# Two weight steps' words are requested earlier at the start of a fused attention and feed-forward kernel

## The chip, the cores and the metric

One core of a Trainium2 chip runs the kernel. The metric is the device time of one execution in microseconds (us). TensorE is called PE here, VectorE DVE, ScalarE ACT, GpSimd POOL and SyncE SP; SP issues every DMA of this kernel, from one queue, in the order in which its instructions stand.

## The reference

Attention with a local window of 32 and 32 global tokens, then LayerNorm, a two-layer feed-forward with ReLU, and a residual (batch 8, 8 heads, 512 local and 32 global tokens, head width 64, model width 512, hidden width 2048):

```python
s_l = concat([scale * q_l @ k_g.T, where(|i - j| <= 32, scale * q_l @ k_l.T, -1e9)])
out_l = softmax(s_l) @ concat([v_g, v_l])          # local rows
out_g = softmax(scale * q_g @ k_all.T) @ v_all     # global rows
x = heads side by side, 8 x 544 rows of 512 
xn = (x - mean) / sqrt(var + 1e-6) * g_ln
out = x + max(xn @ w_ch1, 0) @ w_ch2
```

## The kernel before

The work is cut into chunks of 512 rows (two batch halves of 256 rows each), nine in all; the last holds the global rows. One attention **unit** is one pair of heads in one half, so a chunk has eight units: 1 to 4 give the first half, 5 to 8 the second. The units of the first chunk run alone at the start of the kernel; those of a later chunk run between the feed-forward matmuls of the chunk before.

A unit's steps: its operands `u` come by one DMA (L245, 848 KB); PE makes the scores (L262); DVE adds the mask and takes the row extremes (`p`, `mn`, L275, called the score pass below); ACT takes the exponentials (L285, four to a unit); PE transposes the result (L299) and ACT copies it (`pt`, L301); PE multiplies by the values (L317); DVE scales into `x` (L329). Behind unit 4 and behind unit 8 the half is complete: SP stores it (`xs`, L343), DVE and POOL work out the norm (L189 to L196), ACT (first half, L202) or DVE (second half, L207) applies it, and PE transposes it in four blocks (L493) that ACT and DVE write out as a high and a low part (`xh` L505, `xl` L506).

The feed-forward of a chunk runs over 16 **weight steps**. Step by step, `mm1` (L532) makes 128 hidden columns in 12 matmuls, ACT and DVE write them as two parts (L540, L541), and `mm2` (L551) adds them to the chunk's output one step later. Every weight is kept as two numbers of lower precision, and only during the start and the first chunk are they made: the words of a step (`raw`, 1 MB) come by one DMA (L165), and `split_weights` turns them into high and low parts in seven passes over 128 x 1024 elements: ACT L138 and L139, DVE L141, L142 and L146, ACT L150, DVE L152. L139 works in place on `raw` and waits only for its words; L138 also needs one of two `tmp` buffers. The words of a step lie in a staging buffer that `RAWS` names; step 5 takes that of step 1, step 6 that of step 2, step 7 that of step 3 and step 8 that of step 4, each when L146 of the earlier step has read it.

What sets the order: SP's and (from the first chunk's feed-forward on) PE's instructions are in the order of the code inside a `manual_schedule`. What stands outside the `with` block of the start (the words of step 5 and later, asked for by `split`) is merged into SP's order by the scheduler, which also orders ACT, DVE and POOL from its own estimates; all engines then run their instructions strictly in that fixed order. The start is written with `hurry(True)`, a high priority. `load_weights_to(n)` asks for the words of all steps up to n that weren't asked for yet:

```python
        for n in range(2, need[0]):
            units[n].load()
            if n == 3:
                load_weights_to(1)
...
                if n == HP + 1:
                    load_weights_to(2)
                    units[need[0]].load()
                    units[need[0] + 1].load()
```

`need[0]` is 8 and `HP` is 4. The second place stands behind the values of unit 4, and so behind the store of the first half; the words of steps 3 and 4 are asked for behind the store of the second half (`load_weights_to(4)`).

Of the kernel before, what the change touches and what calls it, by code (L numbers as in the profile page):

```python
# [46 lines left out]
def attention_ffn_kernel(  # L47
# [106 lines left out]
    def weight_stream(ap):  # L154

        ahead = []
        done = [0, 0]

        def load(n):

            for f in range(done[0], min(n, NF)):
                tag = RAWS[f]
                pool = {"w": wpool, "o": fpool}[tag[0]]
                raw = pool.tile([P, KT * P + DM], I64, name="raw", tag=tag)
                nc.sync.dma_start(raw, wd[f])  # L165
                ahead.append(raw)
                done[0] += 1

        def split(n, more=0):

            for f in range(done[1], min(n, NF)):
                load(f + 1)
                w = wpool.tile([P, 2, KT * P + DM], F32R, name="w", tag=f"w{f}")
                wts[f] = w[:, 0], w[:, 1]
                done[1] += 1
                yield from split_weights(ap, ahead.pop(0), *wts[f])
                load(f + 1 + more)

        return load, split
# [406 lines left out]
    def hurry(on):  # L586

        return tc.high_priority() if on else nullcontext()
# [5 lines left out]
    def tiles_of(xs):  # L594
        return [x[:, j, :] for x in xs for j in range(2)]
# [27 lines left out]
    load_weights_to, weights_to = weight_stream(wtmp)  # L623
# [4 lines left out]
    def begin(phase):  # L628
        if pools:
            pools.pop().__exit__(None, None, None)  # L630
        if phase == 2:
            return
        if phase == 1:
            wcm.__exit__(None, None, None)
        cm, ap = open_pool(f"apool{phase}")
        pools.append(cm)
        us = phases[phase]
        for a, b in zip(us, us[1:] + [None]):
            a.ap, a.next = ap, b
        if phase == 1:  # L640
            us[0].load_keys()
            us[0].load_values()
        else:
            us[0].load(2)
            us[1].load()
# [52 lines left out]
    with tc.manual_schedule(engines={ET.SP}):  # L698
        begin(0)
        nc.sync.dma_start(g_sb, g_ln.rearrange("(t p) o -> p (t o)", p=P))  # L700
        for n in range(2, need[0]):
            units[n].load()
            if n == 3:
                load_weights_to(1)
        with hurry(True):
            scores = [u.scores() for u in units[:need[0]]]
            after = {}
            next(scores[0])
            for n in range(need[0] + 2):
                if n < need[0]:  # L710
                    for _ in scores[n]:
                        pass
                if n + 1 < need[0]:
                    next(scores[n + 1])
                if 0 <= n - 1 < need[0]:
                    for _ in units[n - 1].transposes():
                        pass
                if n >= 2:
                    after[n - 2] = values(units[n - 2])

                if n == HP + 1:
                    load_weights_to(2)
                    units[need[0]].load()
                    units[need[0] + 1].load()
                if n == HP + 2:
                    for _ in after[HP - 1]:
                        pass
                if n == HP + 3:
                    for _ in transpose_chunk(tiles_of(ready[0][:1]), xt, 0, 4):
                        pass  # L730
            load_weights_to(4)
            for _ in after[need[0] - 1]:
                pass
            for _ in transpose_chunk(tiles_of([units[need[0] - 1].xn]), xt, 2, 4):
                pass
        for _ in weights_to(SPLIT_AHEAD):
            pass
# [122 lines left out]
```

## Time and profile before

| | us |
|---|---|
| three runs | 986.77, 989.63, 992.0 |
| median | 989.63 |
| the profiled execution's own time | 991.45 |
| its span (first to last instruction) | 989.6 |
| busy in the span: PE, DVE, ACT, POOL | 938.9, 573.7, 316.9, 44.3 |

The busy shares are an average over two very different stages: about 60 us in which the first chunk's attention runs and the weights begin to arrive, and 930 us of feed-forward in which PE hardly stops. In a row of the timeline the first number is the start, the second the duration, and the bracket tells how long the engine was idle just before and what ended that. A column PEclk gives the granted clock of PE, where 1.00 is 2.4 GHz and 0.50 is 1.2 GHz.

### The profile page before, as it was taken

The numbers are of one execution on the slowest core, as the hardware profiler recorded it, in microseconds if no ns is written. First come the engines' busy times: TensorE is split into PE (matmuls) and PEld (weight loads), VectorE is DVE, ScalarE is ACT, GpSimd is POOL, SyncE is SP. The second block draws the span as 40 slices with busy tenths as digits, with TensorE's granted clock in tenths as the row PEclk, the third lists the DMA queues.
The fourth block names the chain that finished last, engine by engine and source line by source line (L and its number), as shares of the span: only waits on it lengthen the run. The fifth ranks groups of instructions, "written<-read, shape, count | busy, mean of one in ns | idle before, by whom it ended". The sixth has DMA issues, their size and how long they took to land.

```text
span 989.6 us, 21066 instructions
## 1 busy us (share of the span) xinstructions
PE 938.9 (95%) x8616; PEld 724.4 (73%) x8616; DVE 573.7 (58%) x1873; ACT 316.9 (32%) x842; POOL 44.3 (4%) x150
## 2 busy tenths in 40 slices
PE   6579999999999999899999999999999989999997
PEld 4357777777767777777777777777777766766796
DVE  4589955666665766666666667666667542222311
ACT  5677843222322223222332232222322131232210
POOL 3000100000000000000000000000000000000000
PEclk9679999999989999999999999999999999999999
DMA  9576642422241323222233214222413244543110
GB/s 360 195 255 205 229 147 59 155 93 75 89 156 47 117 82 113 91 92 72 95 123 92 102 59 156 93 72 93 144 54 123 83 161 145 194 146 136 33 44 22
DMA packets 31872, 118.80 MB, mean 120 GB/s; under 512 B 4256, under 2 KB 6304, under 8 KB 27680
## 3 DMA queue, kind: packets, MB, share of 16 engines
q1 hardware_dynamic: 31776, 117.46, 34.6%
q8 instruction: 68, 1.11, 0.5%
q14 instruction: 28, 0.23, 0.1%
HBM read 99.62 MB, written 17.83 MB: 119 GB/s over the span
## 4 chain that ended last, share of the span: by engine, by line
PE 75%; DMA 8%; DVE 6%; SPq 2%; ACT 1%; issue 1%; POOL 0%; DVEq 0%; ACTq 0%
PE acc L551 33%; PE ph L532 32%; DMA u<-in_eu 4%; PE sc L262 3%; PE sc L317 3%; DMA raw<-in_wd 2%; DMA out<-ob 2%; SPq L560 1%; PE t L493 1%; PE pv L420 1%; DVE tmp L142 1%; DVE tmp L146 1%; PE sc L372 1%; PE t L408 1%; DVE w L152 1%
## 5 line engine op out<-in xcount | busy, mean ns | idle before, releaser
L551 PE MATMUL acc<-w,hh 128*128 128x512 f32 x1088 | 342.0, 395 | 0.0
L532 PE MATMUL ph<-xh,w 128*128 128x512 f32 (+1 forms) x1216 | 314.8, 385 | 0.0
L307 DVE STREAM_TRANSPOSE pt<-p 32x128 f32<-32x128 f32 x768 | 232.2, 302 | 38.2 <-ACT p L285 26.9
L532 PEld LDWEIGHTS ph<-xh,w 128*128 128x128 f32 x1216 | 216.3, 190 | 49.6 <-issue 2.3
L551 PEld LDWEIGHTS acc<-w,hh 128*128 128x128 f32 x1088 | 205.1, 189 | 45.4
L541 DVE SCALAR_TENSOR_TENSOR hl<-ph,hh 128x512 fp32r<-128x512 f32 (+1 forms) x144 | 93.7, 651 | 232.2 <-ACT hh L540 232.1
L551 PE MATMUL acc<-w,hl 128*128 128x512 f32 x544 | 221.8, 408 | 0.5 <-DVE hl L541 0.5
L540 ACT ACTIVATE hh<-ph 128x512 fp32r<-128x512 f32 (+1 forms) x144 | 82.3, 571 | 408.3 <-PE ph L532 408.3
L532 PE MATMUL ph<-xl,w 128*128 128x512 f32 x512 | 142.3, 400 | 0.0
L285 ACT ACTIVATE p<-p,mn 128x128 f32<-128x128 f32 x256 | 100.4, 394 | 126.1 <-DVE mn L275 125.9
L551 PEld LDWEIGHTS acc<-w,hl 128*128 128x128 f32 x544 | 102.2, 188 | 26.0 <-issue 2.6
L532 PEld LDWEIGHTS ph<-xl,w 128*128 128x128 f32 x512 | 97.1, 190 | 25.5 <-issue 1.8
L275 DVE CUSTOM_DVE_ANT_0 p<-sc,mask 128x128 f32<-128x128 f32 x256 | 63.0, 284 | 52.6 <-PE sc L262 46.9
L262 PE MATMUL sc<-u 64*32 64x128 f32 x2048 | 51.7, 297 | 22.5 <-DMA u<-in_eu 18.7
L262 PEld LDWEIGHTS sc<-u 64*32 64x32 f32 x2048 | 31.1, 113 | 46.0 <-issue 37.0
L285 ACT ACTIVATION_READ_ACCUMULATOR p<-p,mn 128x1 f32 x256 | 48.1, 188 | 0.0
L327 POOL TENSOR_SCALAR ri<-sm 128x4 f32<-128x4 f32 x64 | 16.3, 255 | 684.3 <-ACT p L285 680.6
L202 ACT ACTIVATE x<-x,rs 128x512 f32<-128x512 f32 x32 | 24.5, 809 | 54.0 <-DVE rs L196 42.0
L317 PE MATMUL sc<-u,pt 128*32 128x64 f32 x1760 | 37.2, 227 | 0.0
L317 PEld LDWEIGHTS sc<-u,pt 128*32 128x32 f32 x1760 | 28.1, 113 | 11.4 <-issue 11.2
L493 PE MATMUL t<-ident,x 128*128 128x128 f32 x136 | 23.9, 294 | 11.1 <-DVE x L207 3.9
L493 PEld LDWEIGHTS t<-ident,x 128*128 128x128 f32 x136 | 16.9, 147 | 19.0 <-issue 6.7
(61 smaller groups left out, 473.4 us busy)
## 6 DMA issues: line engine op xcount, KB each, us to landing
u<-in_eu SPq DMA_DIRECT2D x63, 848.0 KB, 5.3
raw<-in_wd SPq DMA_DIRECT2D x16, 1024.0 KB, 5.2
gk<-in_gk SPq DMA_DIRECT2D x8, 1088.0 KB, 5.1
xs<-x SPq DMA_DIRECT2D x32, 256.0 KB, 5.7
ob<-xs SPq DMA_DIRECT2D x32, 256.0 KB, 3.7
out<-ob SPq DMA_DIRECT2D x32, 256.0 KB, 2.1
gv<-in_gv SPq DMA_DIRECT2D x8, 1024.0 KB, 4.9
u<-in_eu SPq DMA_DIRECT2D x1, 512.0 KB, 3.7
```

What stands on the lines that cost most here:

```text
L202: nc.scalar.activation(x[:, j, :], x[:, j, :], AF.Identity, bias=rs[:, 1, j:j + 1], scale=rs[:, 0, j:j + 1],)
L262: nc.tensor.matmul(sc[h][gp, qb * P:(qb + 1) * P], self.e[hd, w * WIN:(w + 1) * WIN], self.e[hd, k0 * WIN:(k0 + 4) * WIN], start=True, sto ...
L275: nc.vector.tensor_tensor_reduce(out=self.p[:, c], in0=sc[h][:, qb * P:(qb + 1) * P], in1=masks[half, qb], scale=-QSCALE, scalar=BIG, op0= ...
L285: nc.scalar.activation(self.p[:, c], self.p[:, c], AF.Exp, bias=mn[:, c:c + 1], scale=-1.0, accum_out=self.sm[:, c:c + 1],)
L307: nc.vector.transpose(out=self.pt[rp, :, gp], in_=self.p[gp, :, rp])
L317: nc.tensor.matmul(pv[gp, qb * P + h * D:qb * P + h * D + D], self.pt[:, 2 * h + qb, gp], self.v[:, 4 * qb + g, h * D:(h + 1) * D], start= ...
L327: nc.gpsimd.tensor_scalar(ri, self.sm, SUM_EPS, None, ALU.add)
L493: nc.tensor.transpose(t[:, j * P:(j + 1) * P], xn[j][:, kt * P:(kt + 1) * P], ident)
L532: nc.tensor.matmul(ph[:, :n], w[:, kt, :], xx[kt][:, :n], start=(i == 0), stop=(i == 3 * KT - 1),)
L540: nc.scalar.activation(hh[:, :n], ph[:, :n], AF.Relu)
L541: nc.vector.scalar_tensor_tensor(hl[:, :n], ph[:, :n], 0.0, f32(hh[:, :n]), ALU.max, ALU.subtract)
L551: nc.tensor.matmul(acc[t], a[:, ts], w, start=(f == 0 and i == 0), stop=(f == NF - 1 and i == 2),)
```

## The change

The words of step 2 are asked for right behind the operands of unit 8, and those of step 3 where those of step 2 were, behind the first half's store:

```diff
             units[n].load()
             if n == 3:
                 load_weights_to(1)
+        load_weights_to(2)
         with hurry(True):
             scores = [u.scores() for u in units[:need[0]]]
             after = {}
@@
                 if n == HP + 1:
-                    load_weights_to(2)
+                    load_weights_to(3)
                     units[need[0]].load()
                     units[need[0] + 1].load()
```

The words of step 4 stay behind the second half's store. No instruction is added or taken away on PE, DVE or ACT; what moves is their order. Three places show it. A name's number is that of a buffer: `raw_151` holds the words of step 1 in both kernels, `raw_488` before and `raw_161` now those of step 2, `raw_675` and `raw_490` those of step 3, `raw_677` step 4, `raw_745` step 5, `raw_747` step 6, `raw_804` step 7, `raw_903` step 8.

SP, from the operands of unit 8 (`u_159`) on; `x_283` or `x_285` is the first half, `x_530` or `x_532` the second, and the two `u` behind them belong to the next chunk. Before:

```order
L245 DMA u_159<-in_eu 128x1696
L165 DMA raw_745<-in_wd 128x1024
L343 DMA xs_132<-x_283 128x512 x2
L165 DMA raw_488<-in_wd 128x1024
L245 DMA u_490<-in_eu 128x1696
L245 DMA u_492<-in_eu 128x1696
L165 DMA raw_747<-in_wd 128x1024
L343 DMA xs_132<-x_530 128x512 x2
L165 DMA raw_675<-in_wd 128x1024
L165 DMA raw_677<-in_wd 128x1024
```

Now:

```order
L245 DMA u_159<-in_eu 128x1696
L165 DMA raw_161<-in_wd 128x1024
L165 DMA raw_745<-in_wd 128x1024
L165 DMA raw_747<-in_wd 128x1024
L343 DMA xs_132<-x_285 128x512 x2
L165 DMA raw_490<-in_wd 128x1024
L245 DMA u_492<-in_eu 128x1696
L245 DMA u_494<-in_eu 128x1696
L165 DMA raw_804<-in_wd 128x1024
L343 DMA xs_132<-x_532 128x512 x2
L165 DMA raw_677<-in_wd 128x1024
L165 DMA raw_903<-in_wd 128x1024
```

Step 2's words moved ahead, and with them those of step 6, which now stand ahead of the first half's store, and those of step 7, ahead of the second half's.

ACT, between the copy of unit 4's transposes (`pt_391`, now `pt_393`) and the end of the first half; `p_372` or `p_374` are the exponentials of unit 6, `p_429` or `p_431` of unit 7, `p_504` or `p_506` of unit 8. Before:

```order
L301 COPY pt_391<-tp_392 128x512
L139 ACTIVATE raw_745<-raw_745 128x1024
L285 ACTIVATE p_372,sm_371<-p_372,mn_370 128x128 x4
L301 COPY pt_448<-tp_449 128x512
L285 ACTIVATE p_429,sm_428<-p_429,mn_427 128x128 x4
L301 COPY pt_523<-tp_524 128x512
L202 ACTIVATE x_283<-x_283,rs_479 128x512 x2
L285 ACTIVATE p_504,sm_503<-p_504,mn_502 128x128 x4
L301 COPY pt_562<-tp_563 128x512
L138 ACTIVATE tmp_711<-raw_488 128x1024
L139 ACTIVATE raw_488<-raw_488 128x1024
```

Now:

```order
L301 COPY pt_393<-tp_394 128x512
L138 ACTIVATE tmp_711<-raw_161 128x1024
L139 ACTIVATE raw_161<-raw_161 128x1024
L285 ACTIVATE p_374,sm_373<-p_374,mn_372 128x128 x4
L301 COPY pt_450<-tp_451 128x512
L139 ACTIVATE raw_745<-raw_745 128x1024
L150 CAST w_710<-tmp_711 128x1024
L285 ACTIVATE p_431,sm_430<-p_431,mn_429 128x128 x4
L301 COPY pt_525<-tp_526 128x512
L139 ACTIVATE raw_747<-raw_747 128x1024
L285 ACTIVATE p_506,sm_505<-p_506,mn_504 128x128 x4
L202 ACTIVATE x_285<-x_285,rs_481 128x512 x2
```

Ahead of unit 6's exponentials stand two passes in place of one, ahead of unit 7's two more, and ahead of unit 8's the in-place pass on step 6's words; the two passes of the first half's norm moved from ahead of unit 8's exponentials to behind them, and behind those come `pt_564` and the two passes of step 3 in the place of step 2's. On DVE, step 2's L141, L142 and L146 now stand ahead of unit 7's score pass.

DVE, from the second half's first two blocks to the score pass of unit 9 (`p_751`, the next chunk's first); `tmp_720` belongs to step 3 before, `tmp_737` to step 4, `tmp_796` to step 5. Before:

```order
L506 SCALAR_TENSOR_TENSOR xl0_594<-t_681,g_sb_87,xh0_593 128x256
L506 SCALAR_TENSOR_TENSOR xl0_594<-t_686,g_sb_87,xh0_593 128x256
L141 TENSOR_SCALAR tmp_720<-tmp_720 128x1024
L142 SCALAR_TENSOR_TENSOR tmp_720<-tmp_720,raw_675 128x1024
L506 SCALAR_TENSOR_TENSOR xl2_606<-t_691,g_sb_87,xh2_605 128x256
L506 SCALAR_TENSOR_TENSOR xl2_606<-t_696,g_sb_87,xh2_605 128x256
L146 SCALAR_TENSOR_TENSOR tmp_720<-raw_675,tmp_720 128x1024
L141 TENSOR_SCALAR tmp_737<-tmp_737 128x1024
L142 SCALAR_TENSOR_TENSOR tmp_737<-tmp_737,raw_677 128x1024
L275 ISA p_751,mn_749<-sc_752,mask00_96 128x128
```

Now:

```order
L506 SCALAR_TENSOR_TENSOR xl0_596<-t_681,g_sb_87,xh0_595 128x256
L506 SCALAR_TENSOR_TENSOR xl0_596<-t_686,g_sb_87,xh0_595 128x256
L141 TENSOR_SCALAR tmp_737<-tmp_737 128x1024
L142 SCALAR_TENSOR_TENSOR tmp_737<-tmp_737,raw_677 128x1024
L141 TENSOR_SCALAR tmp_796<-tmp_796 128x1024
L146 SCALAR_TENSOR_TENSOR tmp_737<-raw_677,tmp_737 128x1024
L506 SCALAR_TENSOR_TENSOR xl2_608<-t_691,g_sb_87,xh2_607 128x256
L506 SCALAR_TENSOR_TENSOR xl2_608<-t_696,g_sb_87,xh2_607 128x256
L142 SCALAR_TENSOR_TENSOR tmp_796<-tmp_796,raw_745 128x1024
L152 TENSOR_TENSOR w_736<-tmp_737,w_736 128x1024
L146 SCALAR_TENSOR_TENSOR tmp_796<-raw_745,tmp_796 128x1024
L275 ISA p_751,mn_749<-sc_752,mask00_96 128x128
```

Step 4 is now where step 3 was, and its L146 and the L141 of step 5 moved from behind the last two blocks to ahead of them. On ACT, L138 of step 5 likewise moved ahead of the last two `xh`, and the in-place pass on the words of step 8 (`raw_903`) moved ahead of unit 9's exponentials.

## Rows read from the trace of the kernel before

**Rows 1.** Three stretches of the span: the stretch, its length, then busy us (and instructions) of PE, of PE's weight loads, of DVE, ACT and POOL, the granted clock of PE, the busy share of the DMA engines and their GB/s.

```profile
0.00:60.00 60.00, 34.91 (x593) 21.81 (x594) 30.67 (x111) 36.15 (x97) 12.27 (x54) 0.78 0.70 269
60.00:160.00 100.00, 96.94 (x883) 74.51 (x882) 78.46 (x168) 65.85 (x133) 6.00 (x11) 0.98 0.56 188
160.00:760.00 600.00, 587.82 (x5152) 459.61 (x5151) 393.02 (x1379) 163.84 (x499) 21.34 (x69) 0.99 0.30 98
```

**Rows 2.** The timeline of all engines from the second half's store to the first matmul of the feed-forward.

```profile
48.04 0.80 SPq L343 DMA_DIRECT2D xs<-x  x2
...
54.17 1.12 ACT L138 ACTIVATE tmp<-raw 128x1024 f32<-128x1024 f32 x1 [1.02 <-DMA raw<-in_wd]
...
56.21 0.83 ACT L505 ACTIVATE xh<-t,g_sb 128x256 fp32r<-128x256 f32 x2
56.35 1.23 DVE L142 SCALAR_TENSOR_TENSOR tmp<-tmp,raw 128x1024 int32<-128x1024 int32 x1 [0.34 <-ACT raw L139]
...
57.50 0.87 DVE L506 SCALAR_TENSOR_TENSOR xl<-t,g_sb,xh 128x256 fp32r<-128x256 f32 x2
...
58.03 1.49 PE L262 MATMUL sc<-u 64*32 64x128 f32 x32 [3.55 <-DVE xl L506]
...
59.45 0.80 PE L532 MATMUL ph<-xh,w 128*128 128x512 f32 x1
```

**Rows 3.** The timeline of SP's DMA issues, to 50 us: `u` are units' operands, `raw` a step's words.

```profile
4.17 4.72 SPq L245 DMA_DIRECT2D u<-in_eu  x4
20.74 0.33 SPq L165 DMA_DIRECT2D raw<-in_wd  x1
...
33.04 0.45 SPq L165 DMA_DIRECT2D raw<-in_wd  x1
...
44.21 0.33 SPq L165 DMA_DIRECT2D raw<-in_wd  x1
...
48.89 0.95 SPq L165 DMA_DIRECT2D raw<-in_wd  x2
```

**Rows 4.** DMA issues, by size and by the time from issue to landing (the last number, in us), each asked for one short stretch: 8.5 to 9 us (unit 8's operands), then 20.7 to 21, 33 to 33.4, 44 to 44.5 and 48.8 to 49.3 us (the words of steps 5, 2, 6 and 3).

```profile
u<-in_eu SPq DMA_DIRECT2D x1, 848.0 KB, 16.9
...
raw<-in_wd SPq DMA_DIRECT2D x1, 1024.0 KB, 7.0
...
raw<-in_wd SPq DMA_DIRECT2D x1, 1024.0 KB, 5.1
...
raw<-in_wd SPq DMA_DIRECT2D x1, 1024.0 KB, 4.7
...
raw<-in_wd SPq DMA_DIRECT2D x1, 1024.0 KB, 5.3
```

**Rows 5.** The timeline of ACT: the in-place pass on step 5's words, the first exponentials of units 6 and 7, the norm of the first half, the first exponential of unit 8, and step 2's passes around the first half's blocks.

```profile
27.86 1.10 ACT L139 ACTIVATE raw<-raw 128x1024 int32<-128x1024 uint16 x1 [2.43 <-DMA raw<-in_wd]
28.86 0.39 ACT L285 ACTIVATE p<-p,mn 128x128 f32<-128x128 f32 x1
...
31.29 0.40 ACT L285 ACTIVATE p<-p,mn 128x128 f32<-128x128 f32 x1 [0.32 <-DVE mn L275]
...
35.05 1.52 ACT L202 ACTIVATE x<-x,rs 128x512 f32<-128x512 f32 x2 [1.64 <-DVE rs L196]
36.47 0.39 ACT L285 ACTIVATE p<-p,mn 128x128 f32<-128x128 f32 x1
...
38.47 1.13 ACT L138 ACTIVATE tmp<-raw 128x1024 f32<-128x1024 f32 x1
...
40.53 0.83 ACT L505 ACTIVATE xh<-t,g_sb 128x256 fp32r<-128x256 f32 x2
...
44.26 1.04 ACT L150 CAST w<-tmp 128x1024 fp32r<-128x1024 f32 x1
```

**Rows 6.** The timeline of DVE: the first of four instructions of unit 7's score pass, and step 2's L142.

```profile
30.92 0.26 DVE L275 CUSTOM_DVE_ANT_0 p<-sc,mask 128x128 f32<-128x128 f32 x1
...
40.67 1.23 DVE L142 SCALAR_TENSOR_TENSOR tmp<-tmp,raw 128x1024 int32<-128x1024 int32 x1 [0.35 <-ACT raw L139]
```

**Rows 7.** The timeline of PE: the transposes of unit 6 behind an idle stretch, those of unit 9 behind the first `mm1`, then the second `mm1`, and the scores behind it.

```profile
29.39 1.63 PE L299 MATMUL tp<-ident,p 128*128 128x128 f32 x4 [1.80 <-ACT p L285]
...
64.43 0.72 PE L299 MATMUL tp<-ident,p 128*128 128x128 f32 x4
64.91 1.18 PE L532 MATMUL ph<-xh,w 128*128 128x512 f32 x4
...
67.88 0.67 PE L262 MATMUL sc<-u 64*32 64x128 f32 x32
```

**Rows 8.** What PE waited for between 60 and 160 us: total, times, longest.

```profile
PE tp L299 <- ACT p L285: 1.6, 2, 1.4
PE sc L262 <- DMA u<-in_eu: 0.8, 1, 0.8
PE acc L551 <- DVE hl L541: 0.5, 1, 0.5
```

**Rows 9.** Three short stretches, in the columns of Rows 1.

```profile
20.00:24.00 4.00, 3.80 (x89) 2.54 (x73) 3.07 (x12) 1.73 (x4) 0.75 (x1) 1.00 1.02 422
...
30.00:32.00 2.00, 2.00 (x29) 1.18 (x28) 1.17 (x10) 1.68 (x9) 0.22 (x1) 0.50 0.00 0
...
96.00:104.00 8.00, 6.54 (x30) 4.93 (x29) 7.23 (x17) 7.22 (x15) 0.45 (x1) 1.00 0.75 262
```

## The prediction

> **What bounds the kernel now.** I looked first at where PE stands still. From 160 us on it is busy 98% of the time [rows 1], and the change moves nothing there, so a delay or a gain made earlier is carried to the end unchanged. From 60 to 160 us PE is idle for 3 us in all, and in the first 60 us for 25 us [rows 1]. So the time is decided by when the first feed-forward matmul starts, 59.45 us, and by few waits behind it. Read backwards, what starts it is a chain on ACT and DVE, not on PE: PE's scores of unit 9 waited 3.55 us for the last `xl` of DVE, that came behind an L142 of step 3, that behind ACT's passes on words which landed at 54.17, and those were asked for behind the second half's store at 48.04 [rows 2]. The same pattern stands one half earlier: ACT waited 2.43 us for step 5's words before it could give unit 6 its exponentials [rows 5]. The start is therefore a queue question: what stands ahead of the units' own work on ACT and DVE, and when its words land.
>
> **The change part by part.** All durations are start to start from the rows; I follow the chain forward and write how far each point slips.
>
> *Where step 2's words land.* They are asked for at 8.9, right behind unit 8's operands [rows 3]. Those were issued at 8.5 and took 16.9 us, to 25.4; step 5's words, next in line, were issued at 20.74 and took 7.0, to 27.7 [rows 3, 4], while the DMA engines were full [rows 9]. Step 2's words now have that next place, so they can land with the operands at the earliest, 25.4, and at 27.7 if they merely take step 5's place. I take 27.7, since the bytes ahead of them are the same. Step 5's words move one place back, to 30.0.
>
> The Trainium skill, DMA: Bandwidth & Descriptors (Queues, rings and completion order), says that one copy is split over as many as 16 rings, each worked through in order, and that completion is nevertheless not first in, first out. By that the early end could hold; the sum would be the first rival's, below. The two landings that the rows show are in order, so the trace leans to 27.7.
>
> *Unit 6.* ACT runs L138 and L139 of step 2 (2.06 us, 38.47 to 40.53) in front of its exponentials, where one in-place pass stood (1.00 us) [rows 5]. They begin at 27.8 + 2.06 = 29.9 instead of 28.86: **+1.0**.
>
> *Unit 7.* L142 of step 2 waits on DVE for L139's end at 30.0; L142 needs 1.2 and L146, over as many elements, as much, so unit 7's score pass starts at 32.4 instead of 30.92 [rows 6]. On ACT four exponentials and a copy need 2.0 (36.47 to 38.47), then come step 5's in-place pass (1.0) and step 2's L150 (1.0) [rows 5]: 29.9 + 2.0 + 2.0 = 33.9 instead of 31.29, **+2.6**.
>
> *Unit 8.* Ahead of it is now the in-place pass on step 6's words. They need the buffer of step 2, free at 32.4; alone on the queue they take 4.7 us, as they did before [rows 4], so they land at 37.2. ACT is free of unit 7 at 35.9 and stands idle for 1.3 us. Unit 8's exponentials begin at 38.2 instead of 36.47 [rows 5]: **+1.7**. The norm of the first half (1.42, 35.05 to 36.47) stood ahead of them and now stands behind: 38.2 + 2.0 + 1.4 = 41.6 for L138 of step 3, where L138 of step 2 started at 38.47 [rows 5]: **+3.1**. Step 3's words are not late for that: they stand on SP behind step 6's and the first half's store, which slip by 1.5 with unit 7's score pass, so 33.04 + 1.5 + 5.1 = 39.6 [rows 3, 4].
>
> *The second half.* From here to the second store the order is as before with step 3 for step 2, so the store slips by the same 3.1, and step 4's words, asked for behind it at 48.89 + 3.1 with the landing time of 5.3 [rows 3, 4], land at 57.3, where step 3's landed at 54.2. So nothing of the lead that step 2 has gained shortens this wait: the step that is asked for at the second store is a later one, and ACT waits for it all the same. Then one more L138 stands ahead of the last `xh` on ACT (1.0), and an L141 (one source instead of two, estimated at half of L142, 0.6) and an L146 (1.15) ahead of the last `xl` on DVE. ACT's piece runs beside DVE's, so the larger counts: 3.1 + 1.75 = **+4.9** for the last `xl`, for unit 9's scores and for the first `mm1`, which starts at 64.3.
>
> *Behind the first `mm1`.* It took 5.0 us (59.45 to 64.43), then unit 9's transposes and, at 64.91, the second `mm1` (3.0) followed without a wait [rows 2, 7]. It now ends at 69.3. Unit 9's exponentials have two new pieces ahead of them on ACT: the in-place pass on step 8's words, whose buffer is free only when step 4's L146 ends at 62.4, so that they land at 67.1 (with 4.7) or 67.7 (with 5.3) [rows 4], and step 5's L150. That is 67.4 + 1.0 + 1.0, then the exponentials (the 2.0 above less a copy, estimated at 1.6) and the transposes (0.5): the second `mm1` at 71.5, **+6.6**, with PE idle for 1.6 us in front of the transposes.
>
> *What comes back.* Between 60 and 160 us PE waited 2.9 us: for exponentials 1.6, for a unit's operands 0.8, for `hl` 0.5 [rows 8]. All three stand behind splits on ACT or DVE or behind their words on SP, and the splits are now one step further ahead of PE. That is worth between 0 and 2.9; I take 0.6, the size of the nearest (`hl`, the first in time).
>
> *The clock.* After an idle stretch of 1.8 us at 27.6 to 29.4 the granted clock was 0.50 at 30 to 32; in 96 to 104, where PE was idle for 1.5 us amid feed-forward matmuls, nearly all of it one wait of 1.4, it stayed at 1.00 [rows 7 to 9]. The new pause is 1.6 us long. If the clock falls in it, the second `mm1` takes 5.0 us, as the first, instead of 3.0: 0 to 2.0. I take 0, because the pause stands between feed-forward matmuls, as the second does.
>
> Sum: 6.6 - 0.6 = **+6.0 us**. The profiled execution took 991.45 (span 989.6 and 1.85 around it), so its like would take 997.5. It lay 1.8 above the median of the three runs, 989.63; against the median the forecast is **995.6**.
>
> **The rivals.**
>
> *Step 2's words land with unit 8's operands, at 25.4.* Then ACT starts on them 2.4 us sooner, unit 6 gains 1.3 on before, and unit 8's words and passes come sooner too: step 6's land at 37.2 - 2.3 = 34.9, unit 8's exponentials start at 36.0, L138 of step 3 at 39.4. Every later point slips by 2.3 less: 6.0 - 2.3 = +3.7, 993.3. This decides the verdict: not slower by over 0.5% if they land before about 26.6. For it: it is the earlier issue. Against it: operands and step 5's words landed one behind the other, 2.3 apart [rows 3, 4].
>
> *The lead pays back in full.* All 2.9 us of waits between 60 and 160 us vanish: 6.6 - 2.9 = +3.7, again 993.3. For it: DVE is busy for 78% of that stretch, and a chain through the splits sets when exponentials come [rows 1, 8]. Against it: PE arrives 6 us late, but the exponentials of a unit still stand between passes in a fixed order.
>
> *The start gets shorter.* If step 2's passes fell into time in which ACT waited anyway (2.43 us before 27.86, 1.64 before 35.05), the first half's blocks could start at 38.5 instead of 40.53 [rows 5], a gain of 2.0, and the same at the second half if step 4 did not stand there: together -4.0, and -6.9 with the waits of the rival above: 985.6 to 982.7. The Trainium skill, Trainium Kernel Development and Optimization (Best Practices), asks for just this, to overlap DMA with compute. Against it: in the new order the passes of steps 3 and 4 stand exactly where those of steps 2 and 3 stood, so the gain is taken away again.
>
> *The clock falls in the new pause*: 6.0 + 2.0 = +8.0, 997.6.
>
> **How the numbers follow.** The median is measured here to about 0.5%, as the three runs lie 0.5% apart, so I call within 0.5% (4.95 us, to 994.6) the same. Forecast as worked out 0.54; with the fallen clock 0.12; the early landing 0.18 and the full payback 0.10, both the same but for the upper edge; the shorter start 0.06, of which 0.04 beyond -0.5%. Slower 0.66, same 0.30, faster 0.04. The range has at its low end the early landing together with the payback (+6.6 - 2.3 - 2.9 = +1.4, 991.0) and at its high end the fallen clock with the late landing of step 8's words (+8.6) and 2.3 us for the spread of the runs, the distance of the highest from the median: 1000.5.
>
> **What would show each step right or wrong.** Right: ACT's L138 of step 2 at about 27.8 right before unit 6's exponentials; a wait of ACT for step 6's words before unit 8's; L138 of step 4 waiting for its words near 57; first `mm1` at 64 to 65, second near 71.5 with a wait for exponentials in front of the transposes; from 160 us on the same spacing as before. Wrong: a first `mm1` before 62, or unit 6's exponentials before 28.5, would mean the first rival; a first `mm1` before 59 the third.

## The result, and the profile after

| | before | changed |
|---|---|---|
| median of eight runs each | 988.60 | 996.26 |
| lowest, highest | 984.32, 992.46 | 992.01, 999.23 |
| ratio, 95% interval | | 1.0069, 1.0041 to 1.0097 |
| the profiled execution, its span | 991.45, 989.6 | 996.02, 993.9 |

The changed kernel is 0.69% slower, some 6.8 us of 988.6. Measured again later, with a fresh set of runs of both, the ratio was 1.0053 (1.0026 to 1.0079), 5.3 us.

The timeline of ACT in the changed kernel, from step 2's passes to step 5's, answers to [rows 2, 5]:

```profile
27.61 1.12 ACT L138 ACTIVATE tmp<-raw 128x1024 f32<-128x1024 f32 x1 [1.82 <-DMA raw<-in_wd]
...
29.65 0.39 ACT L285 ACTIVATE p<-p,mn 128x128 f32<-128x128 f32 x1
...
33.63 0.42 ACT L285 ACTIVATE p<-p,mn 128x128 f32<-128x128 f32 x1
...
37.62 1.11 ACT L139 ACTIVATE raw<-raw 128x1024 int32<-128x1024 uint16 x1 [1.86 <-DMA raw<-in_wd]
38.63 0.39 ACT L285 ACTIVATE p<-p,mn 128x128 f32<-128x128 f32 x1
...
41.58 0.56 ACT L301 COPY pt<-tp 128x512 f32<-128x512 f32 x1
42.67 1.15 ACT L138 ACTIVATE tmp<-raw 128x1024 f32<-128x1024 f32 x1 [0.53 <-DMA raw<-in_wd]
...
58.36 1.11 ACT L138 ACTIVATE tmp<-raw 128x1024 f32<-128x1024 f32 x1 [1.00 <-DMA raw<-in_wd]
...
60.40 1.14 ACT L138 ACTIVATE tmp<-raw 128x1024 f32<-128x1024 f32 x1
61.44 0.83 ACT L505 ACTIVATE xh<-t,g_sb 128x256 fp32r<-128x256 f32 x2
```

Read the brackets. ACT waits for words at four of these places, and they are four different steps' words: 2, 6, 3 and 4. At the third, ACT had finished the copy of unit 7's `pt` at 42.14 (41.58 and 0.56) and stood for the last 0.53 us for step 3's words. The first exponentials of units 6, 7 and 8 are 0.8, 2.3 and 2.2 us later than before, and the L138 that stands ahead of the first half's blocks is 4.2 us later (42.67 against 38.47). At the end, two L138, of steps 4 and 5, stand ahead of the last `xh`, where there was one.

SP's queue for the same stretch, answering to [rows 3]. First step 6's words, then the first half's store, step 3's words, the second half's store and step 4's words:

```profile
32.34 0.33 SPq L165 DMA_DIRECT2D raw<-in_wd  x1
33.75 0.81 SPq L343 DMA_DIRECT2D xs<-x  x2
34.60 0.43 SPq L165 DMA_DIRECT2D raw<-in_wd  x1
...
52.25 0.80 SPq L343 DMA_DIRECT2D xs<-x  x2
53.10 0.44 SPq L165 DMA_DIRECT2D raw<-in_wd  x1
```

And their landings (the last number is us from issue to landing), asked for in three short stretches: step 2's words, step 6's, step 3's. They answer to [rows 4]:

```profile
raw<-in_wd SPq DMA_DIRECT2D x1, 1024.0 KB, 18.7
...
raw<-in_wd SPq DMA_DIRECT2D x1, 1024.0 KB, 5.2
...
raw<-in_wd SPq DMA_DIRECT2D x1, 1024.0 KB, 8.0
```

Step 3's words, asked for 2.3 us behind step 6's, took 8.0 us; step 2's in that place had taken 5.1, with no other step's words in flight. The trace of before already held such a pair: step 3's words, asked for behind the second half's store, took 5.3 us [rows 4], and step 4's, asked for right behind them, took 7.3:

```profile
raw<-in_wd SPq DMA_DIRECT2D x1, 1024.0 KB, 7.3
```

The end of the start, on DVE and then on PE, answers to [rows 2, 7]:

```profile
61.68 0.69 DVE L141 TENSOR_SCALAR tmp<-tmp 128x1024 f32<-128x1024 f32 x1
62.29 1.22 DVE L146 SCALAR_TENSOR_TENSOR tmp<-raw,tmp 128x1024 int32<-128x1024 int32 x1
63.42 0.87 DVE L506 SCALAR_TENSOR_TENSOR xl<-t,g_sb,xh 128x256 fp32r<-128x256 f32 x2
...
63.95 1.49 PE L262 MATMUL sc<-u 64*32 64x128 f32 x32 [5.27 <-DVE xl L506]
65.38 2.07 PE L532 MATMUL ph<-xh,w 128*128 128x512 f32 x4
...
70.93 1.48 PE L299 MATMUL tp<-ident,p 128*128 128x128 f32 x4 [0.99 <-ACT p L285]
72.17 1.18 PE L532 MATMUL ph<-xh,w 128*128 128x512 f32 x4
```

PE waits 5.27 us for the last `xl` where it waited 3.55. The first `mm1` starts 5.9 us later than before, the second 7.3. The L141 and L146 ahead of the `xl` are the two passes that stood behind it before.

Stretches of the changed kernel, in the columns of [rows 1]; the last of them goes from its second `hl` (the low part of the hidden columns, L541, 77.88) to its 13th (150.86), with which the feed-forward of the first chunk is three quarters done:

```profile
0.00:60.00 60.00, 33.25 (x560) 20.55 (x560) 31.12 (x110) 36.45 (x96) 13.75 (x54) 0.76 0.74 286
60.00:160.00 100.00, 94.44 (x900) 72.36 (x900) 74.91 (x155) 62.94 (x125) 7.00 (x10) 0.96 0.50 172
160.00:760.00 600.00, 585.68 (x5161) 458.02 (x5150) 392.86 (x1379) 165.54 (x506) 21.70 (x70) 0.99 0.30 99
...
68.00:70.00 2.00, 1.94 (x7) 1.18 (x6) 1.97 (x8) 1.62 (x2) 0.00 (x0) 0.82 0.57 143
70.00:72.00 2.00, 0.95 (x3) 0.41 (x3) 1.89 (x3) 2.00 (x10) 0.00 (x0) 1.00 0.91 381
...
77.90:150.86 72.96, 72.52 (x671) 56.27 (x670) 55.94 (x125) 48.08 (x101) 6.16 (x9) 1.00 0.56 191
```

The same work before, from the second to the 13th `hl`:

```profile
71.00:147.22 76.22, 73.64 (x672) 56.55 (x671) 62.45 (x129) 53.51 (x105) 5.42 (x9) 1.00 0.59 204
```

It took 76.2 us and now takes 73.0, with PE idle for 0.4 us instead of 2.6; the other 1.1 us of the 3.3 lies in PE's busy time (73.64 and 72.52), and no run says why. So of the 7.3 us by which the second `mm1` is late, the 13th `hl` is late by 3.6 only. What PE waited for in the changed kernel, answering to [rows 8]; the first row lies ahead of the first `mm1`:

```profile
PE sc L262 <- DVE xl L506: 5.3, 1, 5.3
PE tp L299 <- ACT p L285: 1.4, 2, 1.0
```

The waits for `u` and for `hl` are gone, and of the waits for exponentials 0.4 is left behind the second `mm1`.

### The profile page after: what moved, and what is told of

Read it like the earlier page. It is cut to its first block, busy times and chain, and to the rows that moved or that the text cites. A ratio compares the mean times of both kernels' runs of the same rounds, so it can differ in the third digit from the quotient of the medians.

```text
span 993.9 us, 21071 instructions
## 1 busy us (share of the span) xinstructions
PE 936.7 (94%) x8616; PEld 722.8 (73%) x8616; DVE 574.4 (58%) x1873; ACT 316.6 (32%) x842; POOL 47.2 (5%) x150
## 4 chain that ended last, share of the span: by engine, by line
PE 81%; DMA 8%; DVE 5%; ACT 3%; SPq 2%; issue 1%; POOL 0%; ACTq 0%; DVEq 0%
PE acc L551 36%; PE ph L532 34%; DMA raw<-in_wd 4%; DMA u<-in_eu 3%; PE sc L262 3%; PE sc L317 3%; PE t L493 1%; DVE pt L307 1%; PE pv L420 1%; SPq L560 1%; PE sc L372 1%; ACT p L285 1%; DMA out<-ob 1%; PE t L408 1%; ACT raw L139 1%
## 5 line engine op out<-in xcount | busy, mean ns | idle before, releaser
L307 DVE STREAM_TRANSPOSE pt<-p 32x128 f32<-32x128 f32 x768 | 232.1, 302 | 38.2 <-ACT p L285 26.9
L541 DVE SCALAR_TENSOR_TENSOR hl<-ph,hh 128x512 fp32r<-128x512 f32 (+1 forms) x144 | 93.9, 652 | 237.2 <-ACT hh L540 237.2
L327 POOL TENSOR_SCALAR ri<-sm 128x4 f32<-128x4 f32 x64 | 20.0, 312 | 685.7 <-ACT p L285 682.0
L317 PEld LDWEIGHTS sc<-u,pt 128*32 128x32 f32 x1760 | 27.7, 111 | 11.1 <-issue 10.7
```

Source lines behind the costliest of these rows:

```text
L307: nc.vector.transpose(out=self.pt[rp, :, gp], in_=self.p[gp, :, rp])
L317: nc.tensor.matmul(pv[gp, qb * P + h * D:qb * P + h * D + D], self.pt[:, 2 * h + qb, gp], self.v[:, 4 * qb + g, h * D:(h + 1) * D], start= ...
L327: nc.gpsimd.tensor_scalar(ri, self.sm, SUM_EPS, None, ALU.add)
L541: nc.vector.scalar_tensor_tensor(hl[:, :n], ph[:, :n], 0.0, f32(hh[:, :n]), ALU.max, ALU.subtract)
```

## The experiments

**The question.** The prediction has the slip come through units 6 to 8: their exponentials stand behind step 2's passes, and what they lose is handed on. Its rivals to be told apart: the early megabyte itself costs, by traffic and by its place in the queue (A); only the request for step 3 at the first half's store costs (B); or it takes both halves of the change, because only then do steps 3 and 4 stand where steps 2 and 3 stood (the theory that I set out with). All results first; the first `mm1` is its start in the profiled execution, and the 13th `hl` the measure of the first chunk's end that the texts below use, with its slip against the first profile of the kernel before.

| kernel | ratio, 95% interval | first mm1 | 13th hl, slip |
|---|---|---|---|
| before, first profile | 1 | 59.45 | 147.22 |
| b2_again (before) | one run, 983.18 us | 58.95 | 144.65, -2.6 |
| changed | 1.0069, 1.0041 to 1.0097 | 65.38 | 150.86, +3.6 |
| a2_again (changed) | 1.0053, 1.0026 to 1.0079 | 65.19 | 150.94, +3.7 |
| e1_early2 | 0.9984, 0.9957 to 1.0011 | 61.26 | 145.77, -1.5 |
| e2_third | 0.9989, 0.9963 to 1.0015 | 59.48 | 147.34, +0.1 |
| e3_hold6 | 1.0034, 1.0004 to 1.0065 | 65.81 | 151.20, +4.0 |
| e4_hold2 | 1.0024, 0.9994 to 1.0053 | 64.42 | 149.40, +2.2 |
| e5_a_hold5 | 1.0046, 1.0021 to 1.0071 | 63.16 | 150.48, +3.3 |
| e6_a_hold4 | 0.9962, 0.9933 to 0.9992 | 60.43 | 144.36, -2.9 |
| e7_a_hold3 | 0.9999, 0.9968 to 1.0030 | 55.72 | 144.71, -2.5 |
| e8_b_hold3 | 0.9939, 0.9911 to 0.9967 | 54.23 | 139.47, -7.8 |
| e9_b_hold4 | 1.0010, 0.9981 to 1.0039 | 56.94 | 142.63, -4.6 |
| e10_b_hold3_again | 0.9923, 0.9890 to 0.9955 | 54.49 | 140.09, -7.1 |

**One half of the change at a time.** e1_early2 has the first added line alone, e2_third the other edit alone:

```diff
# e1_early2, against before
+        load_weights_to(2)
         with hurry(True):
# e2_third, against before
-                    load_weights_to(2)
+                    load_weights_to(3)
```

> The kernel before, with only the first half of the change: the second step's words are asked for behind the first chunk's last unit, and nothing is asked for behind the first half's store. Theory (the slip comes from where the passes of the steps stand in ACT's and DVE's order, and needs both halves, since only then do steps 3 and 4 stand where steps 2 and 3 stood): the last xl of the first chunk and the first mm1 come 0.5 to 1.5 us later than before, not 5.9; step 2's words still land near 27.6 us; time 0 to +1.5 us of the kernel before. Rival A (the 1 MB fetched early is itself what costs, by its traffic and its place ahead of the operands of the last units): the exponentials of units 6 to 8 slip by 0.8 to 2.3 us as in the changed kernel, and the first mm1 by 4 us or more, time +4 to +8 us. Rival B (what costs is only that step 3's words are asked for at the first half's store): 0 us within 0.5.

> The kernel before, with only the second half of the change: nothing is asked for behind the first chunk's last unit, and behind the first half's store the words of the second and the third step are asked for, one behind the other. Theory (it needs both halves): the first mm1 comes 0.5 to 1.5 us later than before, time 0 to +1.5 us. Rival A (the early 1 MB costs): exponentials of units 6 to 8 as in the kernel before, first mm1 within 0.5 us of it, time 0 us. Rival B (asking for step 3 at the first half's store is what costs): first mm1 4 us or more later, time +4 to +8 us.

Neither changes the time. In e1_early2 the timeline shows unit 8's first exponential, the second half's store and the first `mm1`:

```profile
38.79 0.38 ACT L285 ACTIVATE p<-p,mn 128x128 f32<-128x128 f32 x1
...
49.20 0.80 SPq L343 DMA_DIRECT2D xs<-x  x2
...
61.26 2.07 PE L532 MATMUL ph<-xh,w 128*128 128x512 f32 x4
```

Unit 8 is as late as in the changed kernel (38.63), and yet the store is 1.2 us later than before and not 4.2: by themselves the early megabyte and the slip of three units cost 1.2 us at the store and nothing in time, against A. What is missing here is a step whose words are asked for at the first half's store. In e2_third two steps are asked for there, and the first `mm1` stands at 59.48: against B. The first `mm1` slips by 1.8 and by 0.0 us alone and by 5.9 together, so it does take both; my sizes for each alone (0.5 to 1.5) were a little under and a little over.

**Is it unit 8's wait, or step 2's early passes?** Both kernels start from the changed one and hold the two ACT passes of one step behind the last exponential of unit 8, by an order without a wait, since both are on ACT (lines from L138 on are 10 later in all kernels that hold):

```diff
# e3_hold6: HOLD = {5: 'exp'}; e4_hold2: HOLD = {1: 'exp'}   (f is the step less one)
+    def behind(f):
+        if f in HOLD:
+            return tc.issue_after(held[HOLD[f]].ins)
+        return nullcontext()
...
+        with behind(f):
             nc.scalar.activation(tmp, f32(top), AF.Abs, scale=REBIAS)
             nc.scalar.activation(last, third, AF.Copy, scale=THIRD)
```

> The changed kernel, with the two ACT passes of the sixth weight step held behind the last exponential of unit 8, so that this unit no longer waits for the sixth step's words. Theory of the prediction's third term (the wait of 1.86 us for these words ahead of unit 8's exponentials is a link of the chain that ends at the first mm1): the exponentials of unit 8 come about 2 to 3 us earlier than in the changed kernel (near 36 us, not 38.6), but step 3's words, which are asked for at the store, land at the same time, so that the first mm1 gains only about 0.6 us; time 0 to 1 us under the changed kernel. Rival (unit 8's slip passes whole into the second half): the first mm1 gains 2 us or more and so does the time.

> The changed kernel, with the two ACT passes of the second weight step held behind the last exponential of unit 8; its words are fetched as early as in the changed kernel. It parts the early words from the early passes. Theory: units 6 and 7 lose their slip of 0.8 and 2.3 us (exponentials near 28.9 and 31.3 us), but the passes come back behind unit 8, ahead of the last xh, so that the first mm1 stays where the changed kernel has it, within 0.5 us, and so does the time, within 1 us. Rival A (the early traffic costs): units 6 and 7 keep their slip with the passes gone. Rival C (the early passes are the whole cost): the first mm1 falls back by 4 us or more to where the kernel before has it, and the time with it.

In e3_hold6 unit 8's first exponential, step 3's L148 (L138 above) and the first `mm1`, then the landing of step 3's words:

```profile
36.61 0.40 ACT L295 ACTIVATE p<-p,mn 128x128 f32<-128x128 f32 x1 [0.98 <-DVE mn L285]
...
42.95 1.12 ACT L148 ACTIVATE tmp<-raw 128x1024 f32<-128x1024 f32 x1 [1.82 <-DMA raw<-in_wd]
...
65.81 2.00 PE L542 MATMUL ph<-xh,w 128*128 128x512 f32 x4
```

```profile
raw<-in_wd SPq DMA_DIRECT2D x1, 1024.0 KB, 8.5
```

Unit 8 gained its 2 us, and ACT then stood 1.82 us for step 3's words, asked for at 34.47 and landed 8.5 later. So unit 8's wait isn't what sets the second half: with it or without it the words arrive at 42.6 to 43.0. That holds as long as step 2's passes stand early, since the words are asked for behind the first half's store, and DVE writes that half behind these passes (the next kernel moves them). I had expected 0.6 us at the first `mm1`; it gained nothing, and the intervals of its time and of the changed kernel's overlap.

In e4_hold2 the first half's store, step 3's L148, the in-place pass on step 6's words and the first `mm1`:

```profile
29.07 0.81 SPq L353 DMA_DIRECT2D xs<-x  x2
...
39.70 1.17 ACT L148 ACTIVATE tmp<-raw 128x1024 f32<-128x1024 f32 x1
...
46.92 1.13 ACT L149 ACTIVATE raw<-raw 128x1024 int32<-128x1024 uint16 x1 [1.99 <-DMA raw<-in_wd]
...
64.42 2.07 PE L542 MATMUL ph<-xh,w 128*128 128x512 f32 x4
```

With the early words kept and their passes put off, units 6, 7 and 8 start their exponentials at 25.73, 30.68 and 35.67, all ahead of the kernel before, the store comes 3.1 us ahead of it and step 3's words are there in time. Still the first `mm1` is 5.0 us late. Step 2's and step 3's passes now stand together ahead of the first half's blocks, whose `xh` start 1.3 us later than before (41.83 for 40.53). The second half's store is 3.1 us late (51.09), so 1.7 more is lost there: ahead of the copy of unit 8's `pt` now stands the in-place pass on step 6's words, for which ACT waited 1.99 us. The last 1.9 us come behind the store, where step 4's words and step 5's pass still stand ahead of the last `xl`. Rival A of this pair (early traffic) and C (early passes are all) both fall. The first `mm1` came 1.0 earlier than in the changed kernel, twice what I had allowed. Of time, its interval and that of the changed kernel overlap.

**Taking the passes out of the way, one step more at a time.** The theory now is that the slip comes from the passes of steps 3, 4 and 5, and from the words that they wait for, ahead of the last `xl`. Three kernels start from the changed one and hold ACT's passes behind the first chunk's last `xh`, and e8 and e9 do so from the kernel before:

```diff
# held behind the last xh ('xh' in place of 'exp')
e5_a_hold5:  HOLD = {4: 'xh', 5: 'xh'}                                  # steps 5, 6
e6_a_hold4:  HOLD = {3: 'xh', 4: 'xh', 5: 'xh', 6: 'xh'}                # steps 4 to 7
e7_a_hold3:  HOLD = {2: 'xh', 3: 'xh', 4: 'xh', 5: 'xh', 6: 'xh'}       # steps 3 to 7
e8_b_hold3, e10_b_hold3_again: as e7_a_hold3, without the change
e9_b_hold4:  as e6_a_hold4, without the change
```

> The changed kernel, with the ACT passes of the weight steps 5 and 6 held behind the first chunk's last xh, so that no pass of step 5 stands ahead of the last xh and xl. Theory after the first four runs (the first mm1 slips because the passes of steps 3 and 4, and now step 5's, stand ahead of the last xl on ACT and DVE, not because of units 6 to 8): step 5's L138 on ACT and its L141 and the L146 behind it on DVE leave the way, worth 1.0 to 1.8 us; unit 8 no longer waits for step 6's words; the first mm1 comes at 62.0 to 63.8 us in place of 65.4; the slip at the end of the first chunk falls from +3.6 to +0.5 to +2.5 us; time 1 to 4 us under the changed kernel. Rival (the last xl waits for step 4's words alone, so that passes behind them cost nothing): first mm1 and time as in the changed kernel within 0.5 us.

> The changed kernel, with the ACT passes of the steps 4 to 7 held behind the first chunk's last xh, so that the last xh and xl wait for neither the words of step 4 nor any pass of it. Theory: the last xl follows its transposes at once; the first mm1 at 59 to 60.5 us, where the kernel before has it (59.45); the end of the first chunk 0 to 2 us ahead of the kernel before, time -2 to +1 us of it. Rival A (weight preparation that is put off comes back as waits of TensorE for weights, as in the prediction's rival of full payback): first mm1 near 60 but the end of the first chunk still 3 us or more behind the kernel before. Rival B (the early 1 MB or the slip of units 6 to 8 sets it): first mm1 at 63 us or more.

> The changed kernel, with the ACT passes of the steps 3 to 7 held behind the first chunk's last xh: of the second half's weight work nothing stands ahead of the last xl, while the words are still asked for as in the changed kernel. Theory: second store 47 to 48 us (52.3 in the changed kernel), first mm1 at 55.5 to 57 us, 2.5 to 4 us ahead of the kernel before; the end of the first chunk 1 to 3.5 us ahead of it; time -1 to -4 us of the kernel before. Rival A (full payback): first mm1 early, but waits of TensorE for weights grow by as much, time within 1 us of the kernel before. Rival B (units 6 to 8): first mm1 at 63 us or more, time as in the changed kernel.

> The kernel before, with the ACT passes of the steps 3 to 7 held behind the first chunk's last xh, and nothing of the change. Theory: the same cure with no early words, so that units 6 to 8 run early too: unit 8's exponentials near 33.4 us, first mm1 at 53.5 to 55.5 us, 4 to 6 us ahead of the kernel before; the end of the first chunk 2 to 5 us ahead; time -2 to -5 us of the kernel before, a version faster than both. Rival (full payback, since the weights of steps 3 to 7 are the bound of the first chunk): time within 1 us of the kernel before, with longer waits of TensorE for weights between 60 and 160 us.

The first `mm1` of e5_a_hold5:

```profile
63.16 2.02 PE L542 MATMUL ph<-xh,w 128*128 128x512 f32 x4
```

Of e6_a_hold4:

```profile
60.43 2.07 PE L542 MATMUL ph<-xh,w 128*128 128x512 f32 x4
```

Of e7_a_hold3, with the second half's store:

```profile
47.17 0.80 SPq L353 DMA_DIRECT2D xs<-x  x2
...
55.72 2.07 PE L542 MATMUL ph<-xh,w 128*128 128x512 f32 x4
```

The timeline of e8_b_hold3, with its store, last `xl` and first `mm1`:

```profile
45.69 0.80 SPq L353 DMA_DIRECT2D xs<-x  x2
...
52.24 0.91 DVE L516 SCALAR_TENSOR_TENSOR xl<-t,g_sb,xh 128x256 fp32r<-128x256 f32 x2 [0.90 <-ACT xh L515]
...
54.23 2.07 PE L542 MATMUL ph<-xh,w 128*128 128x512 f32 x4
```

The moment of the first `mm1` now comes apart: without step 5's passes 2.2 us earlier, without step 4's and the wait for its words another 2.7, without step 3's and theirs another 4.7, 9.7 in all, and all three landed in the ranges that I had given for it. That is more than the 5.9 us of the change, because the kernel before has the passes of two steps in these places too. Of e5's 2.2 us, 0.45 lie ahead of the second half's store (51.80 for 52.25) and 1.8 behind it; unit 8's exponentials start 2.4 us earlier there, at 36.22, and step 3's L148 still waits 1.57 us for its words, until 42.25. The first chunk's end doesn't follow one for one: 0.4, 6.1 and -0.4 us. e5 still waits 2.0 us for exponentials and 1.3 for a copy of `pt` between 60 and 190 us, e6 1.0, and e7 2.9 and 0.6: put off as far as in e7, preparation comes back as waits there. So e7 gave the time of the kernel before, where I had expected 1 to 4 us less, and its rival of full payback fits the step from e6 to e7. One profile of each shows this, and their intervals of time overlap; of what e7 lost on e6, 2.9 us are its longer wait for `u` at the chunk's end (4.3 us, 1.4 in e6). e6 reached that end 2.9 us ahead of the kernel before, where I had expected 0 to 2, and was 3.8 us faster (0.8 to 6.6 by the interval); e5 won 0.4 us at the chunk's end where I had expected 1 to 3.

e8_b_hold3 is faster than both kernels, by 0.6% of before, with more won at the chunk's end (7.8 us) than the 2 to 5 that I had expected. It holds the same passes as e7, and yet its waits for exponentials are only 0.2 us.

**What was left.** Three questions: is the time beyond the slip of 3.6 us chance, is holding step 3 needed, and does e8's result stand.

> The changed kernel once more, with a second profile. In the first profiles its slip against the kernel before is 3.6 us at the end of the first chunk and 7.7 us a few us later, where PE waits 3.8 us for the transfer of u at the chunk's end (1.3 us in the kernel before) and the granted clock is 0.62 in 192 to 196 us. Theory (this second part is chance of one execution, not the change): the end of the first chunk comes within 0.5 us of where it came in the first profile of the changed kernel, and the wait for u at the chunk's end differs from 3.8 us by up to 2.5 us; time +3 to +7 us of the kernel before. Rival (the change also lengthens the wait for u): 3.8 us again within 0.3 us, and time +6.8 us again.

> The kernel before once more, for a second profile. Theory (the wait for u at the chunk's end is chance): the first mm1 at 59.5 us and the end of the first chunk within 0.5 us of the first profile, but the wait for u at the chunk's end somewhere between 1.3 and 4.3 us, with a lower granted clock behind it where it is over 2 us. Rival: 1.3 us again within 0.3 us, and a clock of 1.00.

> The kernel before, with the ACT passes of the steps 4 to 7 held behind the first chunk's last xh; step 3's passes stay where they were. Holding step 3's passes too made the changed kernel's first mm1 4.7 us earlier but was taken back by waits for weights. Theory (the first chunk is bound by the weight passes once the first mm1 is early, so that the moment of the first mm1 no longer counts): first mm1 at 56 to 57.5 us, about 2 us later than with step 3 held too, but the end of the first chunk within 1.5 us of that kernel's (-7.8 us), time -4 to -7 us of the kernel before. Rival (what counts is the first mm1): the end of the first chunk 2 us or more later than with step 3 held too, time -2 to -4 us.

> The kernel before, with the ACT passes of the steps 3 to 7 held behind the first chunk's last xh, once more, since the kernel that holds only the steps 4 to 7 reached nothing while its first mm1 came just 2.7 us later. Theory (what the first chunk wins is carried to the end): first mm1 within 0.5 us of 54.2, the end of the first chunk 6 to 8.5 us ahead of the first profile of the kernel before, time -3 to -8 us of it. Rival (the first result was chance of a session): end of the first chunk less than 5 us ahead, time within 2 us of the kernel before.

In the second profiles the stretch from the second to the 13th `hl` took this in the kernel before:

```profile
70.56:144.65 74.09, 72.96 (x671) 56.33 (x671) 62.45 (x129) 53.65 (x105) 6.22 (x9) 1.00 0.59 209
```

And this in the changed one:

```profile
77.69:150.94 73.25, 72.78 (x671) 56.38 (x670) 55.93 (x125) 47.79 (x101) 5.82 (x9) 1.00 0.55 190
```

The changed kernel repeats itself (13th `hl` within 0.1 us). The kernel before doesn't: its second execution reached that `hl` 2.6 us sooner than its first, against the 0.5 that I had allowed. Taking the two profiles of each, the slip at the 13th `hl` is 3.7 - (-1.3) = 5.0 us, which lies inside both measured intervals (4.1 to 9.6, and 2.6 to 7.8). The payback is 76.2 - 73.0 = 3.3 by the first pair of profiles and 74.1 - 73.3 = 0.8 by the second, where PE of the kernel before waited in that stretch for exponentials alone (1.0 us) and for no `u`.

Behind it, at the end of the first chunk, PE waits for `u`: 1.28 and 2.01 us in the two profiles of before, 3.77 and 2.85 in those of the changed kernel. That the size varies is shown; whether the change also lengthens it on average, two profiles each can't tell. Behind the 2.01 us the granted clock stayed at 1.00, where I had expected a lower one behind a wait of over 2 us.

e9_b_hold4 misses: its first `mm1` is where I expected it, 2.7 us behind e8's, but the first chunk's end is 3.2 behind e8's, where I had expected 1.5 at most. The rival (what counts is the first `mm1`) has that right, but its time, 2 to 4 us under before, isn't seen either. From the kernel before, step 3's passes must be held too; from the changed kernel, holding them was no gain. I have no run that says why the two differ. e10_b_hold3_again confirms e8: 0.8% under before, first chunk's end 7.1 ahead.

## Why the prediction was right

The number was right, 995.6 forecast and 996.3 measured, and the sign too: +6.0 us forecast, +6.8 and +5.3 by the two measured ratios. The path that it drew was right up to unit 8 and again from the second half's store on; between the two it named the wrong wait. By its own steps:

- **Step 2's words** at 27.7: ACT took them up at 27.61. The first rival, landing with unit 8's operands, is out. The Trainium skill, DMA: Bandwidth & Descriptors (Queues, rings and completion order), on which that rival leaned, allows completion out of order; here step 2's words landed behind unit 8's operands, which were issued before them, and step 3's behind step 6's.
- **Units 6, 7 and 8** at 29.9, 33.9 and 38.2: 29.65, 33.63 and 38.63, with the wait for step 6's words that was foreseen (37.2 forecast, 37.62).
- **"Step 3's words are not late for that"** is the sentence that failed. They were taken to land at 39.6, by 5.1 us, the time of the row of before in that place; they were issued when forecast, 1.6 us later than step 2's before, but took 8.0, with step 6's words issued 2.3 us ahead of them. L138 of step 3 started at 42.67 instead of 41.6: ACT was free at 42.14, 0.5 later than forecast, mostly because unit 8 came 0.4 later, and then stood 0.53 us for the words. Every later point of the start carries this 1.1 us: step 4's words 58.36 for 57.3, the first `mm1` 65.38 for 64.3.
- So **the handing on from unit 8** had nearly the right size but wasn't the wait that ended last. Two paths end within 0.53 us of each other at step 3's L138, the units' first and the words' last. e3_hold6 and e5_a_hold5 took unit 8's wait away and the words held; e1_early2 has all of the units' slip and only 1.8 us at the first `mm1`. No run takes the words' path away alone; by the trace that would win 0.53 us.
- **"The step that is asked for at the second store is a later one"**, and the extra passes ahead of the last `xl` (+1.75): right. In the changed kernel, step 4's words land 4.2 us late with the store, and from there to the last `xl` it is 5.06 us (58.36 to 63.42) instead of 3.33 (54.17 to 57.50), 1.7 more. e5_a_hold5 and e6_a_hold4 priced the two: 2.2 for step 5's passes, 1.8 of it behind the second half's store, and 2.7 for step 4's words and passes.
- **The second `mm1`**: +7.3 for +6.6, with a wait for the exponentials of 1.0 (1.6 forecast). **The clock** was at 0.82 in 68 to 70 us and at 1.00 in 70 to 72, in the pause, and stayed there: 0, as taken.
- **What comes back**: 0.6 taken of 0 to 2.9, and 0.8 to 3.3 measured. It was mis-sized low, by the first pair of profiles above all, where even the upper end is passed. The rival of full payback is in part true: PE had 0.4 us of waits left there.
- **The shorter start** by overlap is out for this change: the time of e1_early2, which has the overlap alone, lies between 0.4% under and 0.1% over that of the kernel before. The Trainium skill, Trainium Kernel Development and Optimization (Best Practices), asks for such overlap; here the words were early and the passes on them stood in front of other work.

That the sum came so close is luck in part, because two sizes were off in opposite directions: the start slipped by 0.7 us more than forecast at the second `mm1`, and 0.2 to 2.7 us more came back. What is left at the 13th `hl` is 5.0 us by two profiles of each kernel, and the two measurements of time say 6.8 and 5.3. That a delay is carried to the end unchanged, as the prediction assumed, no single pair of profiles shows: the first pair is 3.6 us apart at the 13th `hl` and 4.3 at the end of the span, the second 6.3 and 8.5. From there on the traces differ at the chunks' ends, among other things by the waits for `u` told above, which change from one execution of a kernel to the next.

## What to carry to other kernels

When a transfer is asked for sooner, look at what is asked for next in its old place, and what is in flight then: a landing time read from the old trace holds only for the old neighbours (5.1 us alone, 8.0 behind another megabyte). The trace of before had a row for it, the 7.3 us of step 4's words behind step 3's. Fetching early and working early are two decisions; here the work on weights that nobody needed yet stood in a fixed order ahead of the blocks that everything waited for, and holding that work back, with the fetches as they were, won 0.6 to 0.8%, where the change, which moves the work up with the fetches, lost 0.5 to 0.7%. Step 2's fetch and passes moved up alone (e1_early2) changed nothing that the runs can tell. An earlier first matmul is worth only what is not paid back as waits for the work put off: 4.7 us at the first `mm1` were -0.4 at the first chunk's end in one place (e6 to e7), and 2.7 were 3.2 in another (e9 to e8). The first of these rests on one profile of each kernel, and two profiles of the kernel before lie 2.6 us apart at that point; the second is borne out by the times, whose intervals don't meet.

## What the runs showed of the hardware

Two transfers of 1 MB on SP's queue, the second issued 2.3 us behind the first, landed after 5.2 and 8.0 us in the changed kernel; issued one right behind the other they took 5.3 and 7.3 in the kernel before. Where no other step's words were in flight, a step's words took 4.7 us (step 6 before), 5.1 (step 2 before) and 5.5 (step 3 in e4_hold2). In e10_b_hold3_again PE waited 4.2 us for `u` at the end of the first chunk, and the granted clock went from 1.00 to 0.50 behind it:

```profile
172.00:176.00 4.00, 4.00 (x19) 3.06 (x17) 3.23 (x11) 1.16 (x5) 0.23 (x1) 1.00 0.76 257
176.00:180.00 4.00, 0.22 (x1) 0.00 (x0) 2.37 (x8) 0.00 (x0) 0.00 (x0) 0.80 0.44 156
180.00:184.00 4.00, 3.63 (x68) 2.81 (x69) 1.35 (x9) 1.54 (x7) 0.00 (x0) 0.50 0.11 17
184.00:188.00 4.00, 4.00 (x16) 3.24 (x15) 3.60 (x12) 0.82 (x3) 0.22 (x1) 0.85 0.52 204
```

In the first and the second profile of the kernel before, with waits of 1.28 and 2.01 us at that place, it stayed at 1.00; in the changed kernel, with 3.77 us, it was 0.62 in 192 to 196 us. So a transfer that came this late cost there twice, once as a wait and once by the clock. How late it is differs between executions of one kernel (2.1 and 4.2 us in e8 and e10, which are the same), and the two profiles of before end 8.3 us apart, 5.7 of it behind the 13th `hl`.
